# Adding the epsilon to the softmax row sums on ScalarE instead of VectorE

## The chip, the cores and the metric

One Trainium2 chip, one of its cores. The metric is the device time of one execution in microseconds (us). Lower is better.

## The reference

Attention over 4 batches, 8 heads, 576 positions, head size 64, with a learned position bias, followed by a mixture of experts in which each token takes one of 8 experts:

```python
scores = scale * q @ k.T + bias                      # per batch and head
scores = scores - scores.max(-1)
attn = exp(scores)
attn = attn / (attn.sum(-1) + 1e-09)                 # the epsilon that the change moves
x = (attn @ v)                                       # (4, 576, 512) after joining the heads
logits = x @ w_gate                                  # 8 experts
e = argmax(logits) or the token before's expert      # decided by a sigmoid gate, in order of s
out = softmax(logits)[e] * (relu(x @ w1[e]) @ w2[e])
```

## The kernel before, in words

**Position bias (to about 100 us).** A small network is evaluated for all pairs of positions and written to memory, from where each head pair reads its bias rows. The first attention groups run beside it.

**Attention (about 100 to 350 us).** Heads are taken in 4 pairs `p`, batches in 4 `b`, so there are 16 pairs (p, b). Each has 576 query rows in five tiles `qt`: four of 128 rows for each of the two heads, and one that holds the last 64 rows of both. For each unit, `emit_s` lets TensorE compute scores into PSUM, VectorE adds the bias and takes the row extreme (L319), and ScalarE takes the exponential and accumulates the row sum (L324) into `sums`, a tile of 128 partitions by (pair, query tile, batch, head) that lives in SBUF. `emit_t` transposes the exponentials on TensorE (L383) and ScalarE copies them out of PSUM (L389). `emit_av` multiplies by v on TensorE (L414), VectorE copies the product out (L423), and for the last query tile it copies two folded sums into `sums` (L425). Then `emit_recip` adds 1e-9 to the ten sums per partition of this (p, b) (L429) and takes their reciprocal in place (L430). In the next step `emit_out` uses them: `emit_logits_b` (for the last two head pairs) lets TensorE compute expert logits (L525) and VectorE scales them with the reciprocals (L531) and reduces them into `lg` (L535). `emit_rows` transposes the attention rows and scales them (L450 and L455 on VectorE; for the very last pair ten copies on ScalarE, L445), splits them in two 16-bit halves and stores them.

**The hinge.** After the last pair (p = 3, b = 3) the expert gate of batches 2 and 3 follows, `emit_gate`: on VectorE maxima (L587), differences (L589), a sigmoid comparison (L592 to L597), one-hot choices (L601 to L609), and on ScalarE two exponentials (L585, L591). `fk_rows` then transposes the choices on TensorE (L673), ScalarE copies them (L1117), VectorE scans along the tokens (L681, L684), and the slots of every token follow. GpSimd gathers the tokens of a block by them, and the weight loads take the expert's number from them. From here each of 22 blocks of 128 tokens runs two matrix products (L916, L940), each weight being split in a high part (ScalarE, L882) and a low part (VectorE, L889, or GpSimd through `sub_pool`, L112).

**What sets the order.** Each engine executes its own queue in order. Up to the last unit of attention, a planner orders the instructions of each engine by program order and by its own costs of each instruction. The steps after the last unit (`for s in range(NU, NU + LC + 1)`), and the routing after them, stand in `tc.manual_schedule()`: there the order of the program is the order of each queue. In these steps lie the last `emit_recip`, `emit_out` and `emit_gate`, and also `ops10`, the split of a block's first weight, of which the low parts are 16 subtractions on GpSimd.

Of the kernel before, what the change touches and what calls it, by code (L numbers as in the profile page):

```python
# [12 lines left out]
AF = mybir.ActivationFunctionType  # L13
ALU = mybir.AluOpType
# [31 lines left out]
def build(tc, nc, io):  # L46
# [379 lines left out]

    def emit_recip(p, b):
        rv = sums[:, p, :, b, :]
        nc.vector.tensor_scalar(out=rv, in0=rv, scalar1=1e-9, scalar2=None, op0=ALU.add)  # L429
        nc.vector.reciprocal(out=rv, in_=rv)  # L430

    def emit_rows(p, b, u):
# [534 lines left out]
    def step(s):  # L967
# [44 lines left out]
        for u in sorted({s - LC, s - LC0}):  # L1012
            if not 0 <= u < NU or s - u != (LC if groups[units[u][0]][0] else LC0):
                continue
            gi, hh = units[u]
            p, b, qt = groups[gi]
            if qt == QORD[1] and hh == 1 and (p, b) not in DMP:
                emit_av(p, b, 0)
            if qt == 4:
                emit_av(p, b, 1)  # L1020
                emit_recip(p, b)
                late.append((p, b, gi))
# [30 lines left out]
    out = io["out"]  # L1053
# [57 lines left out]
    with tc.manual_schedule():  # L1111
# [20 lines left out]
        for i in range(2):  # L1132
            nc.tensor.matmul(
                out=cn[:, i:i + 1], lhsT=amat16[:, i], rhs=R["cs"][:, S - 1:S], start=True, stop=True
            )
        nc.vector.tensor_scalar(
            out=nbc, in0=c128[0:32, 0:18], scalar1=cn[:, 0:1], scalar2=None, op0=ALU.is_lt
# [3 lines left out]
            out=gp[:, 1], in0=cn[:, 1:2].to_broadcast([32, B]), scalar=-1.0, in1=gmat, op0=ALU.add, op1=ALU.mult  # L1141
# [3 lines left out]
        for i in (2, 3):  # L1145
# [4 lines left out]
            out=ecm[:, K1:], in0=c128[0:8, 0:NB], scalar1=cn[0:8, 3:4], scalar2=None, op0=ALU.is_ge  # L1150
        )
        nc.vector.tensor_tensor(
            out=ez, in0=ecm.unsqueeze(2).to_broadcast([8, NBLK, NE]),
# [17 lines left out]
            out=mkp.rearrange("p k e -> p (k e)"), lhsT=on[0:8, 0:128], rhs=ez.rearrange("p k e -> p (k e)"),  # L1171
# [7 lines left out]
        for b in range(K1, K1 + 2):  # L1179
# [6 lines left out]
            out=mk, in0=mkp, in1=emadd.unsqueeze(1).to_broadcast([128, NBLK, NE]), op=ALU.add  # L1186
# [3 lines left out]
        for b in range(K1, K1 + 2):  # L1190
# [17 lines left out]
            out=i1, in0=sls, scalar1=0.0, scalar2=float(NT // 2 - 1), op0=ALU.is_lt, op1=ALU.add  # L1208
# [153 lines left out]
```

## Time and profile before

| | |
|---|---|
| time, median of 3 runs | 635.19 us (631.98 to 641.85) |
| the profiled execution | 635.78 us, its span 634.0 us |
| mean granted TensorE clock | 0.968 of full speed |
| busy share of the span: TensorE, VectorE, ScalarE, GpSimd | 88%, 81%, 72%, 43% |

The profile records one execution. The span runs from its first to its last instruction. PE is TensorE, DVE VectorE, ACT ScalarE, POOL GpSimd. A row of the timeline is a stretch of like instructions of one engine; "x16" means sixteen of them. L112 is the line of `sub_pool`, whatever calls it, and L118 that of `sub_dve`.

### The profile page before, as it was taken

Reading aid. Unit: us, or ns where it says so; the run is one execution under the profiler, and the core shown is the slowest. Engines: PE = TensorE matmul, PEld = TensorE weight load, DVE = VectorE, ACT = ScalarE, POOL = GpSimd, SP = SyncE. Lnnn points to the kernel's source line nnn. Section 1 sums busy time; section 2 is a strip of 40 time slices with the busy share of each in tenths; the row PEclk is TensorE's granted clock in tenths of the full one; section 3 lists DMA queues with packets and bytes.
Section 4 is the critical chain, followed back from the end, with each engine's and each line's share of the span. In section 5 each row is a group of like instructions: output and inputs, shape, how many; then the busy total and the mean of one; then the engine's idle time right before and its main releaser. Section 6 shows DMA issues by size and latency. Waiting matters only on the chain. (4 is left out here: it accounts for less than half of the span.)

```text
span 634.0 us, 14152 instructions
## 1 busy us (share of the span) xinstructions
PE 559.1 (88%) x5210; PEld 373.0 (59%) x5230; DVE 515.5 (81%) x957; ACT 453.4 (72%) x735; POOL 270.2 (43%) x307
## 2 busy tenths in 40 slices
PE   4767999899889988998999688768989999999993
PEld 1223446566566566774766574655666868686861
DVE  6878885797898988879775787786979999999961
ACT  5777787596777766775877364767678887988860
POOL 5100002970998678665433757211235332523111
PEclk9699999999999999999999869979999999999997
DMA  8665538828987899550750036767975456224301
GB/s 276 212 172 160 157 106 267 263 50 197 249 208 190 204 231 227 114 174 20 262 110 1 20 101 217 275 172 255 276 271 181 146 156 199 78 65 89 53 35 36
DMA packets 101755, 102.57 MB, mean 162 GB/s; under 512 B 69552, under 2 KB 78896, under 8 KB 98098
## 3 DMA queue, kind: packets, MB, share of 16 engines
q1 hardware_dynamic: 96736, 85.89, 49.5%
q0 software_dynamic: 4800, 15.43, 7.2%
q8 instruction: 43, 0.70, 0.5%
q10 hardware_dynamic: 146, 0.30, 0.2%
q14 instruction: 30, 0.25, 0.1%
HBM read 128.90 MB, written 21.45 MB: 237 GB/s over the span
## 5 line engine op out<-in xcount | busy, mean ns | idle before, releaser
L324 ACT ACTIVATE e<-e,st 128x576 f32<-128x576 f32 x144 | 111.6, 776 | 18.2 <-DVE st L319 17.5
L319 DVE CUSTOM_DVE_ANT_0 e<-sps,wb 128x576 f32<-128x576 f32 x144 | 106.6, 750 | 19.0 <-PE sps L300 10.9
L958 POOL DMA_INDIRECT out_dram<-y,odx x22 | 33.1, 1506 | 158.1 <-ACT y L955 143.2
L889 DVE TENSOR_TENSOR wl<-wb,wh 128x2048 bf16<-128x2048 f32 (+1 forms) x44 | 93.0, 2145 | 8.1 <-ACT wh L882 8.1
L882 ACT CAST wh<-wb 128x2048 f16<-128x2048 f32 (+1 forms) x50 | 82.9, 1692 | 13.8 <-DMA wb<-in_w_dram 13.5
L389 ACT COPY eT<-ta 128x512 f32<-128x512 f32 x96 | 54.9, 583 | 37.8 <-PE ta L383 36.2
L299 PE MATMUL sps<-kh,qs 128*128 128x288 f16 x256 | 68.3, 288 | 7.2 <-DVE st L319 5.4
L383 PE MATMUL ta<-c_cpb,e 128*128 128x128 f32 x448 | 70.7, 278 | 1.9 <-ACT eT L389 1.5
L300 PE MATMUL sps<-kl,qs 128*128 128x288 f16 x256 | 67.8, 286 | 0.0
L916 PE MATMUL sps<-xT,wb 128*128 128x128 f16 (+1 forms) x1056 | 64.3, 224 | 3.9 <-ACT wb L882 2.2
L916 PEld LDWEIGHTS <-wb 128*128 128x128 f16 (+1 forms) x1056 | 62.2, 100 | 7.1 <-ACT wb L882 2.6
L414 PE MATMUL av<-eT,vt 128*64 128x320 f32 (+1 forms) x384 | 63.6, 426 | 0.0
L204 PE MATMUL sps<-hd,c_cpa 128*32 128x512 f32 (+17 forms) x352 | 46.8, 532 | 18.6 <-DVE hd L190 10.3
L916 PE MATMUL sps<-xT,wh 128*128 128x128 f16 (+1 forms) x704 | 56.2, 225 | 5.1 <-DMA xT<-xg 5.1
L383 PEld LDWEIGHTS ta<-c_cpb,e 128*128 128x128 f32 x448 | 51.5, 141 | 14.5 <-issue 4.0
L940 PEld LDWEIGHTS <-hhT 128*128 128x128 f16 x352 | 33.5, 98 | 42.2 <-issue 6.1
L889 DVE TENSOR_TENSOR wl<-ws,wh 128x2048 bf16<-128x2048 f32 (+1 forms) x25 | 50.4, 2051 | 5.4 <-ACT wh L882 5.4
L190 DVE TENSOR_SCALAR hd<-tab,bp 128x448 f32<-128x448 f32 (+17 forms) x129 | 50.0, 446 | 4.7 <-PE sps L204 4.6
L916 PEld LDWEIGHTS <-wh 128*128 128x128 f16 x704 | 45.6, 101 | 8.3 <-issue 6.1
L889 DVE TENSOR_TENSOR wb<-ws,wb 128x2048 bf16<-128x2048 f32 (+1 forms) x22 | 45.4, 2096 | 6.1 <-ACT wb L882 5.9
L882 ACT CAST wb<-ws 128x2048 f16<-128x2048 f32 (+1 forms) x26 | 41.3, 1634 | 6.5 <-DMA ws<-in_w_dram 6.5
L940 PE MATMUL yp<-wl,hhT 128*128 128x512 bf16 x156 | 40.8, 379 | 5.1 <-POOL wl L112 2.4
(213 smaller groups left out, 1100.9 us busy)
## 6 DMA issues: line engine op xcount, KB each, us to landing
ws<-in_w_dram SPq DMA_DIRECT2D x44, 1024.0 KB
wb<-in_w_dram SPq DMA_DIRECT2D x44, 1024.0 KB
bias_d<-bv SPq DMA_DIRECT2D x36, 295.5 KB
kf<-in_kt_dram SPq DMA_DIRECT2D x24, 288.0 KB
wb<-bias_d SPq DMA_DIRECT2D x16, 288.0 KB
wb<-bias_d SPq DMA_DIRECT2D x16, 256.0 KB
xrow_d<-xo SPq DMA_DIRECT2D x16, 256.0 KB
vt<-in_vl_dram SPq DMA_DIRECT2D x12, 320.0 KB
```

The source lines that it names most:

```text
L190: nc.vector.tensor_scalar(out=hd[:, 0:n], in0=tab[:, 0:n], scalar1=bp[:, k:k + 1], scalar2=0.0, op0=ALU.add, op1=ALU.max,)
L299: nc.tensor.matmul(out=ps[:, half, 0:288], lhsT=lq, rhs=kh[:, j], start=True, stop=False)
L300: nc.tensor.matmul(out=ps[:, half, 0:288], lhsT=lq, rhs=kl[:, j], start=False, stop=True)
L319: nc.vector.tensor_tensor_reduce(out=e, in0=ps[:, :, 0:288], in1=bsl, scale=-0.125, scalar=1e30, op0=ALU.add, op1=ALU.min, accum_out=st[:, ...
L324: nc.scalar.activation(out=e, in_=e, func=AF.Exp, scale=-1.0, bias=st[:, 0:1], accum_out=sm)
L383: nc.tensor.transpose(out=ta[:, j, :], in_=e[:, o:o + 128], identity=ident)
L389: nc.scalar.copy(out=eTv[:, :, hh, o:o + 128], in_=ta)
L414: nc.tensor.matmul(out=av[64 * x:64 * x + 64, 0:n], lhsT=vt[:, j, 64 * x:64 * x + 64], rhs=eT[:, 2 * j + x, 0:n], start=False, stop=(j == 3),)
L882: nc.scalar.copy(out=wh[:, sl], in_=src)
L889: nc.vector.tensor_tensor(out=wl[:, sl], in0=src, in1=wh[:, sl], op=ALU.subtract)
L916: nc.tensor.matmul(out=hp[:, f // 4, 128 * (f % 4):128 * (f % 4) + 128], lhsT=w[:, o:o + 128], rhs=x[:, kt], start=(i == 0), stop=(i == le ...
L940: nc.tensor.matmul(out=yp, lhsT=x[:, kt], rhs=w[:, 512 * kt:512 * kt + 512], start=(i == 0), stop=(i == len(terms) - 1),)
```

## The change

The addition is issued on ScalarE, as a Copy with a bias of 1e-9, in place, on the same ten elements of each of 128 partitions, once for each of the 16 pairs. The reciprocal behind it stays on VectorE. In the code nothing else is touched.

```diff
     def emit_recip(p, b):
         rv = sums[:, p, :, b, :]
-        nc.vector.tensor_scalar(out=rv, in0=rv, scalar1=1e-9, scalar2=None, op0=ALU.add)
+        nc.scalar.activation(out=rv, in_=rv, func=AF.Copy, bias=1e-9)
         nc.vector.reciprocal(out=rv, in_=rv)
```

## Rows read from the trace of the kernel before

**Rows 1.** Windows: length, busy us (x count) per engine, clock, DMA share, GB/s.
```profile
112.00:340.00 228.00, 213.12 (x1739) 143.16 (x1738) 189.98 (x521) 165.70 (x375) 148.42 (x186) 1.00 0.67 172
...
420.00:634.00 214.00, 197.72 (x2166) 143.47 (x2184) 180.52 (x125) 157.61 (x109) 64.71 (x35) 0.97 0.47 138
```

**Rows 2.** Source lines: min/median/max ns; then the group's busy us, mean ns, idle before.
```profile
L429 DVE TENSOR_SCALAR sums<-sums x16: 155/327/7821, 118.0 to 354.3; 128x10 f32<-128x10 f32 x16
...
L430 DVE RECIPROCAL sums<-sums x16: 201/216/218, 118.8 to 362.2; 128x10 f32<-128x10 f32 x16
...
L429 DVE TENSOR_SCALAR sums<-sums 128x10 f32<-128x10 f32 x16 | 13.3, 832 | 0.1
```

**Rows 3.** Timeline of DVE at the last pair: start us, us, what.
```profile
354.34 7.82 DVE L429 TENSOR_SCALAR sums<-sums 128x10 f32<-128x10 f32 x1
...
362.52 0.28 DVE L531 TENSOR_TENSOR tmb<-av,sums 128x90 f32<-128x90 f32 x1
...
363.50 0.24 DVE L589 TENSOR_TENSOR sh<-lg,mx 128x80 f32<-128x80 f32 x1
...
365.41 0.24 DVE L609 TENSOR_TENSOR fk<-oh,fr 128x80 f16<-128x80 f32 x1
```

**Rows 4.** Timeline of POOL over the same stretch.
```profile
352.05 10.09 POOL L112 TENSOR_TENSOR wb<-ws,wb 128x256 bf16<-128x256 f32 x16
```

**Rows 5.** Window over the last addition alone (columns of Rows 1).
```profile
354.30:362.20 7.90, 4.34 (x63) 4.16 (x60) 7.83 (x3) 0.30 (x2) 7.83 (x13) 0.91 0.00 1
```

**Rows 6.** Timeline of ACT around the last pair.
```profile
350.57 3.88 ACT L882 CAST wb<-ws 128x1024 f16<-128x1024 f32 x4
...
363.95 1.73 ACT L445 ACTIVATE xr<-ta,sums 128x64 f32<-128x64 f32 x8
365.52 0.52 ACT L445 ACTIVATE xr<-tb_r,sums 64x64 f32<-64x64 f32 x2
...
367.57 0.63 ACT L1117 COPY kp<-rpa 32x576 f32<-32x576 f32 x1 [0.83 <-PE rpa L673]
```

**Rows 7.** Source line and group on ACT: like small form; every table load.
```profile
L585 ACT ACTIVATE lt<-lg x3: 212/213/218, 268.3 to 363.2; 128x5 f32<-128x5 f32 x2, 128x10 f32<-128x10 f32 x1
...
L141 ACT ACT_TABLE_LOAD x1 | 1.3, 1283 | 2.0 <-POOL zrow L172 2.0
```

**Rows 8.** Timeline of PE around the last pair.
```profile
354.38 1.28 PE L525 MATMUL av<-c_cpb,xt 128*128 128x32 f32 x10
...
366.09 1.45 PE L673 MATMUL rpa<-ident,fk 128*32 128x128 f16 x10 [7.45 <-ACT xr L445]
```

**Rows 9.** Source lines of the gate on DVE, three gates each: min/median/max ns.
```profile
L589 DVE TENSOR_TENSOR sh<-lg,mx x3: 181/242/662, 267.7 to 363.5; 128x40 f32<-128x40 f32 x2, 128x80 f32<-128x80 f32 x1
...
L595 DVE SCALAR_TENSOR_TENSOR fr<-lt,c_cpb x3: 158/393/678, 269.3 to 364.2; 128x5 f32<-128x5 f32 x2, 128x10 f32<-128x10 f32 x1
...
L597 DVE TENSOR_SCALAR fk<-fr x3: 182/230/701, 269.7 to 364.4; 128x40 f16<-128x40 f32 x2, 128x80 f16<-128x80 f32 x1
...
L608 DVE TENSOR_TENSOR oh<-oh,mo x3: 191/234/682, 270.1 to 365.1; 128x40 f32<-128x40 f32 x2, 128x80 f32<-128x80 f32 x1
...
L609 DVE TENSOR_TENSOR fk<-oh,fr x3: 189/243/548, 270.5 to 365.4; 128x40 f16<-128x40 f32 x2, 128x80 f16<-128x80 f32 x1
...
L618 DVE TENSOR_TENSOR pr<-ex,sm x3: 192/232/678, 270.6 to 365.0; 128x40 f32<-128x40 f32 x2, 128x80 f32<-128x80 f32 x1
```

**Rows 10.** Timelines of POOL and DVE at an earlier pair.
```profile
322.66 2.56 POOL L112 TENSOR_TENSOR wl<-ws,wh 128x256 bf16<-128x256 f32 x4 [9.77 <-ACT wh L882]
...
323.93 0.68 DVE L429 TENSOR_SCALAR sums<-sums 128x10 f32<-128x10 f32 x1
```

**Rows 11.** Waits from 112 to 340 us: total us, times, longest.
```profile
ACT eT L389 <- PE ta L383: 30.6, 29, 2.5
...
DVE xt L423 <- PE av L414: 13.4, 10, 2.7
```

**Rows 12.** The page's group of exponentials: busy us, mean ns, idle before.
```profile
L324 ACT ACTIVATE e<-e,st 128x576 f32<-128x576 f32 x144 | 111.6, 776 | 18.2 <-DVE st L319 17.5
```

## The prediction, before the change was run

> **What bounds the kernel now.** I read the busy time by stage first. From 112 to 340 us, the attention, PE is busy 213.1 of 228.0 us and DVE 190.0; from 420 us on, the expert blocks, PE 197.7 of 214.0 us [rows 1]. Both are held by PE, so an addition of ten elements a partition should matter in neither. Then I read the changed line itself. Its sixteen instructions take 155 ns at best and 327 ns in the median, but 7821 ns once; they sum to 13.3 us [rows 2]. So 7.8 us lie in one instruction, and 13.3 - 7.8 = 5.5 us in the other fifteen.
>
> The timeline shows the one: it is the last pair, from 354.34 to 362.16 us [rows 3]. On POOL sixteen subtractions run back to back from 352.05 to 362.14 [rows 4]. The addition ends 0.02 us behind the last of them, and an operation of 0.155 us can have no other reason for 7.8 us: it waited for something that POOL held. In this stretch ACT is busy 0.30 us of 7.90, DMA moves nothing, and PE does 4.34 us and stops [rows 5]. Everything behind it is in written order: reciprocal, logits, gate, token choice. So these 7.8 us are on the path that sets the end, at the hinge where attention ends and routing starts.
>
> What POOL held is not everything on DVE: the reciprocal, behind the same addition, never took more than 218 ns [rows 2]. The Trainium skill, SBUF — State Buffer, "Who interferes with whom", has a rule that fits: VectorE shares one pair of SBUF ports with GpSimd, taken by one-source operations in a fast mode and by those with two SBUF inputs, and whichever engine starts first holds it for its whole instruction. By that rule the wait would have been at most one subtraction; the row shows twelve, so here the measurement decides.
>
> **The change, part by part.**
>
> *Fifteen earlier additions leave DVE.* They cost it 5.5 us. DVE itself waits for PE's product 13.4 us there, ACT for transposes 30.6 us [rows 11], so most of the time is only handed to a later wait. Bounds 0 and 5.5 us; I take 0.9 us, about a sixth, near the lower end since PE is 93% busy [rows 1].
>
> *Sixteen additions come to ACT.* The nearest form, a small ACTIVATE of 128x10, takes 212 to 218 ns [rows 7]: 16 x 0.22 = 3.5 us of ACT. Fifteen stand in attention, where ACT's waits for PE (30.6 us) cover them: cost 0 if covered, 15 x 0.22 = 3.3 us if every one pushes a copy or an exponential. I take 0. The Copy needs no table switch if it is like the copies there now: the whole trace holds one table load, at the beginning [rows 7]. No DMA moves, and the queues of SP and POOL are not passed. The Trainium skill, ScalarE: Activation LUTs, "Rules for kernel authors", speaks against the move: additions belong on VectorE. Its formula of 186 ns + 0.833 ns an element gives an estimate of 194 ns against the 155 ns on VectorE, some 0.6 us over sixteen, if all lay on the path.
>
> *A wait is added:* the reciprocal on DVE now waits for ACT. In attention the bias addition L319 mostly stands between the copy of the sums and the reciprocal, and covers it; queued behind the reciprocal are L450 and later L319s, for which the exponentials wait. Taken as 0, bounded below under the rivals.
>
> *The last pair.* ACT's casts end at 350.57 + 3.88 = 354.45 [rows 6]; the addition would end at about 354.7 and the reciprocal at 354.9. What is late next is PE: L531 needs L525, which ends at 354.38 + 1.28 = 355.66 [rows 8]. So L531 starts at 355.7, not 362.52, and L589, 0.98 us behind it [rows 3], at 356.7 instead of 363.50: 6.8 us earlier.
>
> But now the gate runs under the same subtractions, which it did not before. How much of the 6.8 us does it give back? The second of the three gates ran beside POOL's work: six of its operations show their maximum there. Against their minima they lose 0.48 + 0.52 + 0.52 + 0.49 + 0.36 + 0.49 = 2.86 us [rows 9]. None waited longer than one POOL operation. From the start of L589 to the end of L609 the gate takes 365.65 - 363.50 = 2.15 us undisturbed [rows 3]. So L609 would end at 356.7 + 2.15 + 2.86 = 361.7, 3.9 us earlier.
>
> Behind it, PE's L673 waited before for ACT's ten copies L445, which end at 365.52 + 0.52 = 366.04, and only then did its ten matmuls in 1.45 us [rows 6, 8]. With L589 over at about 357.2 these copies are over 2.3 us later, at 359.5, ahead of L609. So only the last five matmuls, half of 1.45, stand behind L609: they end at 362.4 instead of 367.54. ACT's L1117 and the scans follow 5.1 us earlier. From there the same work follows on the same queues; POOL has finished by then. I see nothing that gives it back: the expert blocks are held by PE from a start that routing sets.
>
> **Sum:** -5.1 - 0.9 + 0 + 0 = -6.0 us against the profiled execution's 635.8 us (634.0 us of span and 1.8 around it), so 629.8 us. That execution lies 0.6 us above the median of the runs, 635.19, which themselves spread by 9.9 us.
>
> **The rivals.**
>
> *The wait moves by one.* L589 or a neighbour is held through the rest of POOL's subtractions, as L429 was, until 362.14. L589 would end at 362.4 instead of 363.74: 1.4 us gained, and 0.9: 633.5 us. For it: the same sixteen subtractions, the same engine, and the one such hold in the trace is at this very place. Against it: L429 in an earlier pair met four like subtractions and got through behind one of them, in 0.68 us [rows 10], and the other fifteen average 5.5 / 15 = 0.37 us. Chance 0.25.
>
> *No contention at all.* The gate needs 2.15 us from 356.7; PE's L673 then waits for the ten ACT copies to 359.3 and ends at 360.7, 6.8 us earlier; with 0.9 us it is 628.1 us. For it: the minima of the gate's operations [rows 9] are this short; against it, the second gate beside POOL was not. Chance 0.06.
>
> *The reciprocal waits for ACT in attention (slower).* If the planner puts the addition behind an exponential of 0.78 us [rows 12], DVE stands still for up to 0.78 + 0.22 = 1.0 us at each of fifteen pairs, and the next bias addition, its exponential and PE's transposes come later by as much: +15 - 5.1 = 645.7 us. It decides for slower from 5.1 / 15 = 0.34 us a pair that reach PE. For it: ACT is busy 165.7 of 228.0 us [rows 1]. Against it: both engines wait for PE just there [rows 11]. Chance 0.16, mostly at its smaller prices, 636 to 641 us.
>
> *It does nothing that shows:* routing comes earlier but a weight load or a gather sets the start of the expert blocks anyway; 634.9 us with the 0.9 alone. Against it: DMA idles through the whole hold [rows 5]. Chance 0.08.
>
> **How the numbers follow.** The forecast, with a gate that gets through behind single subtractions, has 0.45. The predicted time is 629.8 us. Its own range is 627 to 633, from the bounds of the attention terms. For 8 in 10 I take 625 to 638: below, the free gate with more of the 5.5 us; above, the moved wait, the lost gain and the smaller prices of the added wait. A measurement of this kernel can tell some 2% (12.7 us) from no change. Faster by that, under 622.5, needs more than the free gate and all 5.5 us together (635.8 - 6.8 - 5.5 = 623.5): 0.04. Slower by that, over 647.9, needs the added wait beyond its full price: 0.05. Within: 0.91.
>
> **What would show it.** In the trace after: an ACT instruction of 0.2 us on L429 at 354.5 and the reciprocal right behind; gate operations of 0.5 to 0.7 us under POOL's subtractions, none of several us; L1117 about 5 us earlier against the end of the last attention product; no new idle time of DVE in front of L430. Wrong would be one gate operation of about 5 us ending with POOL's last subtraction, or idle time of DVE released by ACT ahead of the reciprocals, or an attention that ends at another time by more than 2 us.

## The result and the profile after

The changed kernel took 627.62 us in the median of four runs (625.56 to 633.02). The kernel before took 638.52 us on the same chip (631.98 to 644.28, four runs). The ratio is 0.986, with a 95% interval of 0.9813 to 0.9907. Run again beside other kernels (e13, below), it gave 0.9925 (0.988 to 0.9969). These ratios are reckoned from the fast executions alone (in e4, below, one of 3008.93 us is left out) and so are not the quotients of the medians. The change makes the kernel faster by about 1%, which is within the 2% that the forecast counted as no change. The time lies inside the forecast's range, but it did not come about in the way forecast.

The profiled execution took 625.56 us, its span 623.8 us. The page of the changed kernel, busy us with its share of the span and the number of instructions:

```profile
span 623.8 us, 14156 instructions
...
PE 557.2 (89%) x5210; PEld 372.8 (60%) x5230; DVE 507.3 (81%) x941; ACT 455.7 (73%) x751; POOL 272.3 (44%) x307
```

The changed line and what stands around its instructions, after (source view: ns min/median/max; then idle time of its engine and of those that waited for it, us and times):

```profile
L429 ACT ACTIVATE sums<-sums x16: 195/213/216, 113.5 to 346.8; 128x10 f32<-128x10 f32 x16
...
  DVE sums L425: 9.2, 6
...
  DVE sums L430: 1.1, 3
```

The 13.3 us of [rows 2] became sixteen times about 0.21 us on ACT. ACT stood 9.2 us in front of them until the sums were there, and DVE stood 1.1 us in all behind them. Now the last pair, timeline of DVE after, answering to [rows 3]:

```profile
346.57 0.14 DVE L425 COPY sums<-av 64x2 f32<-64x2 f32 x1
347.05 0.22 DVE L430 RECIPROCAL sums<-sums 128x10 f32<-128x10 f32 x1 [0.34 <-ACT sums L429]
348.11 0.28 DVE L531 TENSOR_TENSOR tmb<-av,sums 128x90 f32<-128x90 f32 x1 [0.84 <-PE av L525]
...
349.09 5.55 DVE L589 TENSOR_TENSOR sh<-lg,mx 128x80 f32<-128x80 f32 x1
354.56 0.16 DVE L592 TENSOR_SCALAR lt<-lt 128x10 f32<-128x10 f32 x1
...
356.31 0.24 DVE L609 TENSOR_TENSOR fk<-oh,fr 128x80 f16<-128x80 f32 x1
...
359.14 1.34 DVE L681 TENSOR_TENSOR_SCAN e<-kp,rpa 32x576 f16<-32x576 f32 x1 [0.72 <-ACT kp L1117]
```

And of POOL after, answering to [rows 4]:

```profile
342.95 1.54 POOL L112 TENSOR_TENSOR xo<-xr,xo 128x512 bf16<-128x512 f32 x2 [2.03 <-ACT xo L465]
344.45 10.09 POOL L112 TENSOR_TENSOR wb<-ws,wb 128x256 bf16<-128x256 f32 x16
```

L429 no longer waits, but L589, 0.24 us undisturbed [rows 3], takes 5.55 us and ends at 354.64, 0.10 us behind the last subtraction (344.45 + 10.09 = 354.54). Behind it the gate runs undisturbed. The wait has moved by one instruction of its kind.

To see what that was worth, the path from the last copy of sums (L425) to the first scan (L681) is measured in both. Before, on DVE:

```profile
354.17 0.14 DVE L425 COPY sums<-av 64x2 f32<-64x2 f32 x1
...
368.23 1.34 DVE L681 TENSOR_TENSOR_SCAN e<-kp,rpa 32x576 f16<-32x576 f32 x1 [0.71 <-ACT kp L1117]
```

That is 14.06 us before and 12.57 us after: 1.5 us gained at the hinge. The attention, from the first of the sixteen L425 to the last, took 237.0 us before (117.18 to 354.17) and 233.3 us after (113.31 to 346.57): 3.7 us gained. Together 5.2 us. The spans differ by 10.2 us; 3.9 of the rest lie ahead of the first L425 and 1.1 behind L681 (265.8 against 264.6 us to the end). Neither belongs to the change: the second execution of the changed kernel (e13) had its first L425 at 115.22 and 268.0 us behind L681, while its attention and hinge were again 233.3 and 12.57 us. Over all the traces below the first L425 lies between 113.3 and 118.3 us, whatever the edit. Ahead of the attention a part of the difference shows in the granted clock of TensorE, 0.61 of full speed before and 1.00 after in this stretch (windows as in [rows 1]; first before, then after):

```profile
16.00:32.00 16.00, 12.08 (x55) 3.44 (x56) 13.66 (x32) 12.13 (x25) 2.19 (x6) 0.61 0.64 208
```

```profile
16.00:32.00 16.00, 10.32 (x65) 3.28 (x66) 14.43 (x36) 13.55 (x28) 2.19 (x6) 1.00 0.76 246
```

### The profile page after: what moved, and what is told of

Same layout as the page of the kernel before. It is cut to its first block, busy times and chain, and to the rows that moved or that the text cites. A ratio compares the mean times of both kernels' runs of the same rounds, so it can differ in the third digit from the quotient of the medians.

```text
span 623.8 us, 14156 instructions
## 1 busy us (share of the span) xinstructions
PE 557.2 (89%) x5210; PEld 372.8 (60%) x5230; DVE 507.3 (81%) x941; ACT 455.7 (73%) x751; POOL 272.3 (44%) x307
## 5 line engine op out<-in xcount | busy, mean ns | idle before, releaser
L889 DVE TENSOR_TENSOR wl<-wb,wh 128x2048 bf16<-128x2048 f32 (+1 forms) x44 | 92.9, 2146 | 5.5 <-ACT wh L882 5.4
L882 ACT CAST wh<-wb 128x2048 f16<-128x2048 f32 (+1 forms) x50 | 82.9, 1693 | 10.9 <-DMA wb<-in_w_dram 10.6
L916 PE MATMUL sps<-xT,wb 128*128 128x128 f16 (+1 forms) x1056 | 66.6, 227 | 3.0 <-ACT wb L882 1.9
L916 PEld LDWEIGHTS <-wb 128*128 128x128 f16 (+1 forms) x1056 | 64.3, 102 | 6.3 <-ACT wb L882 2.3
L204 PE MATMUL sps<-hd,c_cpa 128*32 128x512 f32 (+17 forms) x352 | 43.7, 492 | 18.3 <-DVE hd L190 9.4
L916 PE MATMUL sps<-xT,wh 128*128 128x128 f16 (+1 forms) x704 | 54.3, 220 | 2.9 <-DMA xT<-xg 2.8
L889 DVE TENSOR_TENSOR wl<-ws,wh 128x2048 bf16<-128x2048 f32 (+1 forms) x25 | 50.5, 2051 | 7.0 <-ACT wh L882 7.0
L889 DVE TENSOR_TENSOR wb<-ws,wb 128x2048 bf16<-128x2048 f32 (+1 forms) x22 | 45.3, 2094 | 5.8 <-ACT wb L882 5.7
L916 PEld LDWEIGHTS <-wh 128*128 128x128 f16 x704 | 43.8, 98 | 6.2 <-issue 3.8
L882 ACT CAST wh<-ws 128x2048 f16<-128x2048 f32 (+1 forms) x26 | 41.5, 1636 | 7.2 <-DMA ws<-in_w_dram 7.2
L940 PE MATMUL yp<-wh,hhT 128*128 128x512 f16 x176 | 43.1, 387 | 4.1 <-ACT wh L882 4.1
```

Source lines behind the costliest of these rows:

```text
L882: nc.scalar.copy(out=wh[:, sl], in_=src)
L889: nc.vector.tensor_tensor(out=wl[:, sl], in0=src, in1=wh[:, sl], op=ALU.subtract)
L916: nc.tensor.matmul(out=hp[:, f // 4, 128 * (f % 4):128 * (f % 4) + 128], lhsT=w[:, o:o + 128], rhs=x[:, kt], start=(i == 0), stop=(i == le ...
L940: nc.tensor.matmul(out=yp, lhsT=x[:, kt], rhs=w[:, 512 * kt:512 * kt + 512], start=(i == 0), stop=(i == len(terms) - 1),)
```

## The experiments

Two questions were open. Why was one instruction held through twelve POOL subtractions, when others pass between two of them? And why did the attention gain 3.7 us? The names used below:

- **Theory S**: the hold comes from an operation on 64 partitions directly ahead of the subtractions. POOL's row "xo<-xr,xo 128x512 ... x2" hides one: its second form is 64x128, the `lo` of the last 64 rows of pair (3, 2). Its rivals: the subtractions alone do it, or the place, or the held instruction's own form.
- **Theory O**: the attention gains because the planner, with other costs to reckon with, puts instructions in another order. **Theory D**: it gains because DVE has 5.5 us less to do and to wait for [rows 2].

The kernel before has the same row, directly ahead of the subtractions that start at 352.05 [rows 4]:

```profile
350.54 1.54 POOL L112 TENSOR_TENSOR xo<-xr,xo 128x512 bf16<-128x512 f32 x2 [2.03 <-ACT xo L465]
```

All runs in one table. A step is the time from one L425 to the next. "Hinge" is the last L425 to the first scan L681, "attention" the first to the last L425, "from 5th" the fifth to the last L425, "two gaps" the sum of the steps from the 8th to the 9th and from the 10th to the 11th L425, all in us of the profiled execution. The runs were taken in three groups (e1 to e4, e5 to e8, e9 to e13), each beside its own executions of the kernel before, whose medians were 639.57, 639.29 and 637.81 us; so medians of different groups compare by their ratios.

| run | median us | ratio to before (95%) | hinge | attention | from 5th | two gaps |
|---|---|---|---|---|---|---|
| before (first profile) | 638.52 | 1 | 14.06 | 237.0 | 190.9 | 36.6 |
| after (first profile) | 627.62 | 0.986 (0.9813 to 0.9907) | 12.57 | 233.3 | 187.5 | 33.3 |
| e13 after again | 633.27 | 0.9925 (0.988 to 0.9969) | 12.57 | 233.3 | 187.4 | 33.5 |
| e1 last only | 637.58 | 0.9989 (0.9949 to 1.003) | 12.58 | 240.8 | 191.6 | 36.1 |
| e2 fifteen only | 633.88 | 0.9914 (0.988 to 0.9948) | 14.08 | 233.6 | 188.0 | 33.0 |
| e3 after, half sub on DVE | 629.56 | 0.9844 (0.9794 to 0.9893) | 8.22 | 233.8 | 187.9 | 33.2 |
| e4 before, half sub on DVE | 635.19 | 0.9927 (0.9888 to 0.9965) | 8.22 | 236.3 | 190.6 | 36.4 |
| e5 no add | 631.57 | 0.9888 (0.9829 to 0.9947) | 12.56 | 232.7 | 187.2 | 33.3 |
| e6 no add, half sub on DVE | 627.63 | 0.9835 (0.9784 to 0.9885) | 8.21 | 232.8 | 186.8 | 33.3 |
| e7 one-element add on DVE | 638.63 | 0.9987 (0.9935 to 1.004) | 12.57 | 238.7 | 190.6 | 35.1 |
| e8 e6, half of the split on DVE | 627.42 | 0.9825 (0.9779 to 0.987) | 6.85 | 234.7 | 189.5 | 33.0 |
| e9 resync | 628.97 | 0.9841 (0.977 to 0.9913) | 8.38 | 234.5 | 188.7 | 33.2 |
| e10 skew in the second run | 630.89 | one run | 8.21 | 232.7 | 187.6 | 33.4 |
| e12 extra DVE op | 634.51 | 0.9912 (0.9869 to 0.9955) | 12.58 | 236.6 | 191.3 | 36.2 |

The first four steps took 45.1 to 49.3 us together, and not by the edit: 45.8 and 45.9 in two executions of the changed kernel, but 46.1 before, 49.3 in e1 and 48.1 in e7, whose queues have there the order of before. The column "from 5th" leaves them out. In e2, e8 and e9 the twelfth step ran at a granted clock of 0.93 and took 25.0 to 25.1 us; in the other eleven it ran at 1.00 and took 23.7 to 24.4 us.

### e1 and e2: the change in two parts

```diff
# e1: the addition on ScalarE for the last pair alone; e2: for the fifteen others alone (!=)
-        nc.scalar.activation(out=rv, in_=rv, func=AF.Copy, bias=1e-9)
+        nc.scalar.activation(...) if (p, b) == (NP - 1, B - 1) else nc.vector.tensor_scalar(...)
```

> Only the last pair's addition is on ScalarE; every queue is otherwise that of the kernel before. Measure: start of L425 of the last pair to start of the scan L681 (14.06 us before, 12.57 after). Theory (the hinge gives only what the moved wait leaves): L589 is held 5.5 us to the end of the sixteen POOL subtractions, the measure is 12.6 us, the time 1.5 us below the kernel before (ratio 0.998). Rival (the whole gain of some 10 us sits in this one instruction): the measure or the end falls by 8 us or more, ratio 0.987.

> The fifteen earlier additions are on ScalarE, the last one on VectorE; every queue is otherwise that of the kernel after. Measure: first to last L425, the attention (237.0 us before, 233.3 after). Theory (the attention gained by the order that the planner made of it and by freed VectorE time): 233.3 us again, the last L429 held 7.8 us, time 3.5 to 4.5 us below the kernel before (ratio 0.993 to 0.995). Rival (the two profiles differ in the attention by chance of execution): 237 us, ratio 0.999 to 1.001.

With the last addition alone on ACT, L589 was held, as in the changed kernel:

```profile
357.13 5.56 DVE L589 TENSOR_TENSOR sh<-lg,mx 128x80 f32<-128x80 f32 x1
```

With the fifteen others alone, L429 was held, as before:

```profile
349.61 7.82 DVE L429 TENSOR_SCALAR sums<-sums 128x10 f32<-128x10 f32 x1
```

The two parts add up: the last addition is worth 1.5 us of hinge; the fifteen are worth 3.4 us of attention. In e1 the attention took even 240.8 us, but the excess lies in the first four steps; from the fifth L425 on it took 191.6 us against 190.9 before. The larger part of the gain is that of the fifteen, of which least was expected.

### e3 and e4: the 64-partition subtraction taken off GpSimd

```diff
-                (sub_pool if (p, b) == (NP - 1, B - 2) else sub_dve)(lo, r[0], hi)
+                (sub_pool if (p, b) == (NP - 1, B - 2) and r[0].shape[0] == 128 else sub_dve)(lo, r[0], hi)
```

> The kernel after, with one POOL subtraction of 64 partitions (0.42 us, L112 on xo of pair 3, 2), the last before the sixteen subtractions, moved to VectorE, which is idle there. Theory S (an operation on half of the partitions leaves the two halves of POOL out of step, so that through the sixteen subtractions the shared ports are never free at one moment): no gate operation takes over 0.9 us, L425 to L681 takes 8.5 to 9.5 us instead of 12.57, the time is 3 to 4 us below the kernel after. Theory Q (sixteen subtractions back to back hold the ports by themselves): L589 is held about 5 us again, L425 to L681 is 12.2 to 12.6 us, the time that of the kernel after within 0.5 us.

> The kernel before, with the same one subtraction of 64 partitions moved from POOL to VectorE. Theory S: L429 of the last pair takes under 0.9 us, L425 to L681 about 9 us instead of 14.06, the time 5 us below the kernel before (ratio 0.992). Theory Q: L429 is held 7.4 to 7.8 us, L425 to L681 is 13.6 to 14.1 us, ratio 0.999 to 1.001.

POOL and then DVE in e3: the same sixteen subtractions, and the longest operations of the gate under them.

```profile
347.78 1.16 POOL L112 TENSOR_TENSOR xo<-xr,xo 128x512 bf16<-128x512 f32 x1 [2.02 <-ACT xo L465]
348.93 10.63 POOL L112 TENSOR_TENSOR wb<-ws,wb 128x256 bf16<-128x256 f32 x16
```

```profile
351.41 0.14 DVE L425 COPY sums<-av 64x2 f32<-64x2 f32 x1
...
353.93 0.24 DVE L589 TENSOR_TENSOR sh<-lg,mx 128x80 f32<-128x80 f32 x1
354.09 0.64 DVE L592 TENSOR_SCALAR lt<-lt 128x10 f32<-128x10 f32 x1
...
356.62 0.71 DVE L608 TENSOR_TENSOR oh<-oh,mo 128x80 f32<-128x80 f32 x1
357.36 0.59 DVE L609 TENSOR_TENSOR fk<-oh,fr 128x80 f16<-128x80 f32 x1
...
359.63 1.33 DVE L681 TENSOR_TENSOR_SCAN e<-kp,rpa 32x576 f16<-32x576 f32 x1
```

In e4, the kernel before with this edit alone, L429 gets through as well:

```profile
351.92 0.58 DVE L429 TENSOR_SCALAR sums<-sums 128x10 f32<-128x10 f32 x1
```

One POOL operation of about 0.4 us (1.54 against 1.16 us) decides it. Without it no operation waits longer than about one subtraction (10.63 / 16 = 0.66 us), and the hinge takes 8.22 us in both, a little under what Theory S foretold (8.5 to 9.5 in e3, about 9 in e4): 4.3 us less than after, 5.8 less than before. So e4 gains as much at the hinge, with the addition still on DVE, as the change and e3 together.

How much of this reaches the end is less certain. From L681 to the end the eight executions with a hold at the sixteen took 264.6 to 268.5 us, the five without one (e3, e4, e6, e8, e9) 267.7 to 270.6. Some of the gain may be given back there. The medians of e5 and e6, which differ by this edit alone, lie 3.9 us apart, so most of it stays.

### e9 and e10: the hold ended, and the hold made

e9 leaves the 64-partition subtraction on GpSimd and adds two copies of two elements behind it, of which the second, on 128 partitions, waits for the first.

```diff
+                if (p, b) == (NP - 1, B - 2) and r[0].shape[0] == 64:
+                    nc.gpsimd.tensor_copy(out=scr[0:64, 0], in_=lo[:, 0:2])
+                    nc.gpsimd.tensor_copy(out=scr[:, 1], in_=scr[:, 0])
```

> The changed kernel, with two tiny copies on GpSimd behind the subtraction on 64 partitions, ahead of the sixteen subtractions: one on 64 partitions, one on all 128 that needs the first one's result and waits for it. The subtraction on 64 partitions stays on GpSimd. Theory (what a 64-partition operation leaves behind, two parts of GpSimd out of step, is what holds VectorE, and a wait of GpSimd for its own result ends it): no operation of the gate over 0.9 us, the last copy of sums to the first scan in 8.2 to 8.7 us. Rival (the hold comes with any 64-partition operation ahead of the sixteen, whatever stands between): L589 held 4.5 to 6 us to the end of the sixteenth subtraction, 12.2 to 12.9 us from copy to scan.

POOL in e9, then the longest operations of the gate on DVE (L613 is L608 of the others):

```profile
346.10 1.54 POOL L112 TENSOR_TENSOR xo<-xr,xo 128x512 bf16<-128x512 f32 x2 [2.03 <-ACT xo L467]
347.71 0.18 POOL L470 CAST scr<-xo 64x2 f32<-64x2 bf16 x1
347.95 0.18 POOL L471 COPY scr<-scr 128x2 f32<-128x2 f32 x1
348.10 10.61 POOL L112 TENSOR_TENSOR wb<-ws,wb 128x256 bf16<-128x256 f32 x16
```

```profile
352.25 0.39 DVE L594 TENSOR_TENSOR sh<-lg,mx 128x80 f32<-128x80 f32 x1
352.56 0.64 DVE L597 TENSOR_SCALAR lt<-lt 128x10 f32<-128x10 f32 x1
...
355.08 0.70 DVE L613 TENSOR_TENSOR oh<-oh,mo 128x80 f32<-128x80 f32 x1
```

e10 does the opposite. It is e6 (no hold; below), with an idle operation on 64 partitions put among the next twelve subtractions, where no instruction was held before.

```diff
+        nc.gpsimd.tensor_tensor(out=scr, in0=ident[0:64], in1=iota[0:64], op=ALU.subtract)
```

> The kernel without the epsilon and with the 64-partition subtraction on VectorE (which had no hold), and a new 64-partition operation on GpSimd put in the middle of its next twelve subtractions (9.0 us, behind the scans), where VectorE lost no more than one subtraction at a time so far. Theory (a 64-partition operation directly ahead of back-to-back subtractions makes the hold): at least one VectorE operation behind it is held to the end of that run, 2.5 to 6 us, and the end comes 1 to 5 us later. Rival (the hold belongs to the sixteen subtractions at the hinge, or to what the moved subtraction did there otherwise): no VectorE operation over 0.9 us in that stretch.

POOL and DVE in e10, and the same instruction (L1148) on DVE in e6:

```profile
357.12 3.60 POOL L112 TENSOR_TENSOR wl<-wb,wh 128x256 bf16<-128x256 f32 x4 [0.66 <-ACT wh L883]
360.68 0.62 POOL L1121 TENSOR_TENSOR scr<-c_cpb 64x128 f32<-64x128 f32 x1
361.27 5.04 POOL L112 TENSOR_TENSOR wl<-wb,wh 128x256 bf16<-128x256 f32 x8
```

```profile
361.25 5.08 DVE L1150 TENSOR_SCALAR gp<-c_cpb,rpb 32x4 f16<-32x4 f32 x1 [0.22 <-PE rpb L1149]
```

```profile
361.80 0.33 DVE L1148 TENSOR_SCALAR gp<-c_cpb,rpb 32x4 f16<-32x4 f32 x1 [0.22 <-PE rpb L1147]
```

An operation on four elements a partition was held 5.08 us, to 366.33; the eight subtractions end at 366.31. It is another place, another line and another form. From L681 to the end e10 took 272.6 us against 267.7 in e6; that is one execution of each. Theory S holds: the hold can be taken away in two ways and was made on purpose in one. An idle operation on 128 partitions in the place of e10's was not tried; but in e9 a short one of 128x2 stands directly ahead of the sixteen, with no gap behind it, and made no hold. That two parts of GpSimd run out of step behind a 64-partition operation, so that one of them always holds the ports, is not seen in a trace; it is inferred, and e9 is what it foretells.

The condition has a limit, seen in the kernel before. Its second gate (284 to 290 us) ran beside 64-partition subtractions too, timeline of POOL:

```profile
285.08 2.95 POOL L112 TENSOR_TENSOR qs<-qf,qs 64x288 f16<-64x288 f32 x4
288.12 1.30 POOL L115 TENSOR_SCALAR kh<-kf 128x576 f16<-128x576 f32 x2
```

They end at 288.03, and 0.09 us pass before the operation on 128 partitions; nothing was held there beyond one operation [rows 9]. In e9 such gaps stand behind the 64-partition operations as well (347.64 to 347.71, 347.89 to 347.95), while at the holds the next operation follows with none (344.49 and 344.45 after, 361.30 and 361.27 in e10). That the gap is a wait that ends the hold there too fits, but was not tried.

### e5 and e6: no addition at all

The addition is left out (at these sums of 1 and more, 1e-9 does not change a 32-bit sum); e6 has the edit of e3 as well.

```diff
-        nc.scalar.activation(out=rv, in_=rv, func=AF.Copy, bias=1e-9)
```

> The addition is left out on every pair (the row sums are at least 1, so 1e-9 does not change them in this precision); the 64-partition subtraction stays on POOL. Theory D (the attention gained by the VectorE time and port waits that the fifteen additions had taken): first to last L425 takes 233 to 234 us, as with the addition on ScalarE, L425 to L681 of the last pair 12.2 to 12.6 us with L589 held, ratio 0.989 to 0.991. Rival O (the gain was a lucky order that the planner made with the addition on ScalarE): this third order takes 236 us or more, ratio 0.995 to 0.999.

> No addition, and the 64-partition subtraction of pair (3, 2) on VectorE. Theory S: no hold, L425 to L681 takes 7.9 to 8.3 us, 4.4 us below the kernel after; with theory D the time is 9.5 to 10.5 us below the kernel before, ratio 0.984 to 0.986. Rival: the gate is held, ratio 0.990.

e5 is the bound of any place for the addition: hinge 12.56 us, L589 held 5.55 us, attention 232.7 us. The change reaches it within noise. So the addition on ACT costs nothing that shows, and what is left at the hinge is the hold; without it, e6 took 8.21 us at the hinge, as foretold by Theory S. By its expectation e5 met Theory D. But the order that the planner made in it is near that of the changed kernel, as told below for L340, so it does not separate the two theories.

### e7: DVE's time taken back without another order

```diff
# against the kernel before: one of the ten elements
-        nc.vector.tensor_scalar(out=rv, in0=rv, scalar1=1e-9, scalar2=None, op0=ALU.add)
+        nc.vector.tensor_scalar(out=rv[:, 4, 1:2], in0=rv[:, 4, 1:2], scalar1=1e-9, scalar2=None, op0=ALU.add)
```

Nine of ten sums get no epsilon.

> The addition stays on VectorE, but on one of the ten sums of a partition alone (the other nine are left as they are); every queue has the order of the kernel before up to about 280 us. An operation on one element should not need the shared ports. Theory D: each L429 takes 0.15 us or less, first to last L425 takes 233 to 235 us in the old order, and the last L429 isn't held but L589 is, 5.5 us; ratio 0.989 to 0.992. Rival O: L429 is as short, but the attention takes 236 to 241 us as before; only the hinge gains its 1.5 us, ratio 0.997 to 0.999.

The line in e7:

```profile
L429 DVE TENSOR_SCALAR sums<-sums x16: 136/148/154, 119.1 to 357.2; 128x1 f32<-128x1 f32 x16
```

DVE's instructions stand in the order of the kernel before. The sixteen additions cost 16 x 0.148 = 2.4 us in place of 13.3, and none waits. The attention took 238.7 us all the same, and the ratio is 0.9987. From the fifth L425 on it took 190.6 us against 190.9 before: the two gaps are 1.5 us shorter and the other steps 1.2 us longer. This was against the theory I favoured: the time and waits that DVE was freed of gained 0.3 us there, not 3.5. e5 has no addition and e7 one of 2.4 us in all that never waits; what else differs between them is the order of the queues: 187.2 against 190.6 us. So Theory D does not explain the gain.

### e12: DVE's time given back with the addition on ScalarE

```diff
         nc.vector.reciprocal(out=rv, in_=rv)
+        if (p, b) != (NP - 1, B - 1):
+            nc.vector.tensor_scalar(out=scr, in0=rv, scalar1=1e-9, scalar2=None, op0=ALU.add)
```

> The changed kernel, with an extra VectorE addition on the same ten sums behind the reciprocal at each of the fifteen earlier pairs, into a tile that nobody reads: it puts back on VectorE what the change took from it in attention, with the addition still on ScalarE and an order of the queues near that of the changed kernel. Theory O (attention gained by the planner's other order): first to last L425 in 232.5 to 234.5 us. Theory D (it gained by VectorE's freed 5.5 us): 236 us or more.

> The changed kernel once more, beside the others on the same chip. L589 held 5.55 us again, 12.5 to 12.6 us from the last copy of sums to the first scan, first to last L425 in 232.5 to 234 us, ratio 0.983 to 0.993.

e13 met its expectation. e12 did not meet that of Theory O: 236.6 us, and taken alone the number is Theory D's. The trace shows why it doesn't separate the two: the extra instruction changed the planner's order too. In the step from the 8th to the 9th L425, DVE issues two subtractions L340, whose transposed halves PE's L354 needs. DVE and PE in the kernel before:

```profile
206.49 1.34 DVE L340 TENSOR_TENSOR e<-e,e 128x1152 f16<-128x1152 f32 x1
209.11 1.80 DVE L340 TENSOR_TENSOR e<-e,e 128x1152 f16<-128x1152 f32 x1
```

```profile
224.25 0.50 PE L354 MATMUL av<-eT,v 128*128 128x256 f16 x3 [1.18 <-DMA eT<-e]
```

In the changed kernel:

```profile
199.77 1.55 DVE L340 TENSOR_TENSOR e<-e,e 128x1152 f16<-128x1152 f32 x1
204.82 1.39 DVE L340 TENSOR_TENSOR e<-e,e 128x1152 f16<-128x1152 f32 x1
```

```profile
216.82 0.49 PE L354 MATMUL av<-eT,v 128*128 128x256 f16 x3
```

In e12:

```profile
204.28 1.35 DVE L341 TENSOR_TENSOR e<-e,e 128x1152 f16<-128x1152 f32 x1
206.91 1.81 DVE L341 TENSOR_TENSOR e<-e,e 128x1152 f16<-128x1152 f32 x1
```

```profile
222.22 0.50 PE L355 MATMUL av<-eT,v 128*128 128x256 f16 x3 [1.35 <-DMA eT<-e]
```

Before and in e12 the two start 2.6 us apart, and PE waits over a microsecond for the transposes; after, they start 5.05 us apart, the first earlier in the order, and PE does not wait. e1, e4 and e7 have the first pattern (3.0, 2.6, 2.6 us), e2, e5 and e13 the second (5.05). In e7 PE's L354 did not wait in this step, and yet the step took 17.9 us, between the 18.6 to 18.9 of the others with the first pattern and the 16.8 to 17.3 of those with the second; so this wait is not the whole of the difference. The columns split in the same way: with an addition that the planner counts on DVE at the earlier pairs, the two gaps take 35.1 to 36.6 us and the attention from the fifth L425 on 190.6 to 191.6; without, 33.0 to 33.5 and 186.8 to 189.5. An instruction of 0.16 us at each of fifteen pairs is not a likely cause of 2.0 us (18.8 against 16.8) in one step and 1.0 (17.4 against 16.4) in another, where the other steps differ by up to 1.1 us in either direction. With e5 and e7, this speaks for the order. A run that holds the changed kernel's order and gives DVE its time back was not made, so that part of Theory O stays inferred; whether a single move of L340 does it is open.

### e8: less of the split on GpSimd

```diff
# against e6
-    ops10 = split_ops(1, 0, on_pool=ALL4)
+    ops10 = split_ops(1, 0, on_pool=((1, 0), (1, 1)))
```

> As e6, and eight of the sixteen POOL subtractions ahead of the gate done as two of 1024 elements on VectorE, which is idle 3.4 us there. POOL is then through some 3 us earlier, about when the gate starts. Expected: gate operations near 0.24 us with at most three of them waiting, L425 to L681 6.5 to 7.5 us instead of 8.2, the time 1 to 1.5 us below e6. Rival: the two operations of some 1.1 us delay the copy L423 of the last pair by more than they save; the time is that of e6 or 1 us above.

Two subtractions L889 went to DVE just ahead of its last copies:

```profile
348.94 2.34 DVE L889 TENSOR_TENSOR wb<-ws,wb 128x1024 bf16<-128x1024 f32 x2
351.21 0.47 DVE L423 COPY xt<-av 128x320 f32<-128x320 f32 x1
351.61 0.14 DVE L425 COPY sums<-av 64x2 f32<-64x2 f32 x1
```

The hinge fell by another 1.4 us, to 6.85. L423 now came without an idle moment, but that cost little: the last step of the attention took 14.57 us against 14.29 in e6. So about 1.1 us should be left. The time, 627.42 us against 627.63, does not show it, and executions of one kernel spread by more than that (625.76 to 629.43 us in e8); neither the expectation nor its rival is decided. That the attention of e8 ended 1.9 us later than that of e6 is for the most part its twelfth step, 25.1 us at the lower clock against 23.7. These two kernels are the fastest of all; their intervals overlap with those of e3 and e9, which compute everything.

## Why the prediction was right and wrong

**Right.** The time, 627.62 us against 629.8, and "same". The addition on ACT (0.213 us in the median against 0.22 taken), directly behind the casts at 346.81, no cost in ACT's queue that shows (187.5 us from the fifth L425 on, 187.2 in e5 without any addition); L531 bound by PE's L525 (0.84 us idle ahead of it); the reciprocal's added wait, 0.34 us at the hinge and 1.1 us in all, so nothing of the 15 us of the slower rival. From L681 to the end nothing is seen to be given back: 265.8 us before, 264.6 and 268.0 in two executions after.

**Wrong: the step from L589 to L609.** The forecast let the gate get through behind single subtractions ("None waited longer than one POOL operation") and gave it 5.1 us. The rival "the wait moves by one", held at 0.25, is what happened: 1.5 us gained, 1.4 in the rival, 5.1 in the sum. The prediction's own sign of being wrong came, an operation of 5.55 us that ended with POOL's last subtraction. The evidence against that rival came from other conditions: the four subtractions of [rows 10] began behind 9.77 us of idle time and the operations of POOL beside the second gate [rows 9] behind a gap, whereas the sixteen followed a 64-partition operation without one. The sixteen subtractions were read [rows 4], what stood in front of them was not. With the hold gone (e3), the forecast's own mechanism gives 14.06 - 8.22 = 5.8 us at the hinge, and the gate's operations take 0.16 to 0.71 us, as [rows 9] had them.

**Wrong: the term for the fifteen additions.** 0.9 us was taken, within 0 to 5.5; measured 3.7 (3.4 in e2). Its reason was wrong too: DVE's time gained nothing that shows (e7), and the gain goes with the planner's order (e5, e7), which is inferred and not tried alone. That order was described ahead of the prediction, but no term was given to it.

So 1.5 + 3.7 stands for 5.1 + 0.9: two errors of about 3.6 and 2.8 us of opposite sign, which the time alone would have hidden. That the time came out so near is luck, and twice: in e13, beside executions of the kernel before of 637.81 us in the median, the same kernel took 633.27 us, outside the forecast's own range of 627 to 633. That range is also narrower than the bounds it is said to come from: -5.1 with 0 to 5.5 us gained and 0 to 3.3 us lost in the attention gives 625.2 to 634.0.

**On the rule of the ports.** The row of before showed twelve subtractions where the rule (the Trainium skill, SBUF — State Buffer, "Who interferes with whom": the engine that issues first has the shared ports for its whole instruction) allows one. e3, e4 and e9 agree with the rule, at most 0.71 us, and the held rows do not. The Trainium skill, GPSIMD Engine Reference, "Instruction dispatch", says that consecutive GpSimd instructions are no barrier between its cores, each of which serves 16 partitions and goes on when its share is done, and that a wait on the first one's completion is one. With that the runs agree: in an operation on 64 partitions the cores have unequal shares, and the hold ended behind the wait of e9. That the cores then stay out of step through the run is inferred; no trace shows a single core.

## What to carry to other kernels

When one short VectorE instruction lasts until the end of a run of GpSimd's, look at the GpSimd instruction ahead of the run, with its forms apart, before moving the victim: moving it handed the wait here to the next instruction that needs the ports. In this kernel it helped to give a 64-partition operation there to another engine, or to put a wait behind it (e3, e4, e9). And where a planner orders the queues, an edit of one cheap instruction can be an edit of the order: test it with a kernel that changes the cost and keeps the order, as e7 does.

## What the runs showed of the hardware

- A VectorE operation was held through the rest of a run of GpSimd subtractions, 7.82, 5.55 and 5.08 us, each time with a 64-partition GpSimd operation ahead of the run and no gap behind it; without it, or with a GpSimd wait of its own result between (two copies of 0.18 us), no more than 0.71 us in those gates.
- GpSimd itself was quicker while it held VectorE off: 10.09 us for the sixteen subtractions, against 10.6 us where VectorE got in between (e3, e6, e9).
- In the held stretches the reciprocal and the one-element addition (136 to 154 ns in e7) never waited.
- Two executions of the same changed kernel differed by 5.3 us in span (623.8 and 629.1), with the same 233.3 and 12.57 us in attention and hinge: parts of a trace compare more closely than whole times here, if one looks at the granted clock of each (1.4 us in one step at 0.93).
